# Attention and two gated MLPs on one core: three token blocks of 704, 768 and 832 in place of 768 each

## The chip, the core and the metric

The kernel runs on one core of a Trainium2 chip. The metric is device time in microseconds (us), the median of the runs shown. The core has five engines that run their own instruction streams and wait for one another by semaphores: PE (matmul), DVE (vector), ACT (scalar), POOL (general) and SP, which here issues almost every DMA, in program order.

## The reference

Attention over 4 batches x 8 heads of 576 queries and keys, head size 64, with a threshold: scores below the row's maximum minus tau are dropped before the softmax. Its output is reshaped to 2304 tokens x 512, and two gated MLPs (the code calls them moe) follow, the first with an RMS normalisation in front:

```python
scores = scale * (q @ k.T)
scores = where(scores >= max(scores) - tau, scores, -1e9)
x = softmax(scores) @ v                      # -> 2304 x 512
x = mlp(rmsnorm(x) * rms_g); x = mlp(x)
# mlp: g = x @ w_gate; (g * sigmoid(g) * (x @ w_val)) @ w_out,  512 -> 1536 -> 512
```

## The kernel before

**Tokens and blocks.** The kernel holds everything transposed: features on partitions, tokens along the free dimension. The 2304 tokens (batch by batch, 576 each) go in three blocks of 768. A block needs all 8 heads of its tokens, so `PHASES` cuts the queries: block 0 takes batch 0 and the first 192 queries of batch 1, block 1 the other 384 of batch 1 and 384 of batch 2, block 2 the rest. For each of four head pairs and each such piece the queries of both heads are laid end to end and cut into tiles of 128 rows (`queries`, `PLAN`): 48 tiles per block. Where a head's rows are no multiple of 128, one tile serves two heads.

**Two attention paths.** Block 0's tiles go first and alone, on a quick path (`fast`): products in plain f32, softmax on DVE, ACT and POOL, transposes on PE, product with V. It works in steps of two tiles (128 queries of either head) or, at the end of a piece whose length is an odd multiple of 64, one tile of 64 queries of either head. The tiles of blocks 1 and 2 (`tile_ops`, `pv`) run beside the MLPs on a split path: q, k and v are cut into parts whose products PE takes at full rate, the probabilities are written as two f16 halves, transposed by DMA, and multiplied with V in groups of query columns (`GROUPS`), nine full products and six of half height per group.

**MLPs.** Per block and MLP there are 18 weight units: 12 of gate and value columns (`gate_val`) and 6 of output columns (`outp`). Every product is made of three products of split parts, so a unit is 48 matmuls of half a block's width HT = 384 columns (`dense`, L923). In the last block 22 of the 24 gate-and-value units use a scheme with seven products in place of eight (`gate_val7`, L955; weights in `weights7`), which needs eight combinations of the activations (`combine`), kept in buffers that earlier served attention (`TS`).

**Weights.** In block 0 they come as 64-bit numbers and are converted on ACT and DVE and split (`weights`, `w_split`). They are then stored in DRAM for the later blocks, either as both parts (1024 KB) or, for units in `K_E`, as the unsplit f32 (512 KB) that is split again on reload. Units of the seven-product scheme need the unsplit copy as well.

**Order.** The program's operations are collected with a cost, a due time and their dependences, and a list scheduler (`order`) writes out the order for each engine. Due times come from constants (`T0`, `UP`, `FP`, `OFF`, `OFFF`, `LEAD` ...); tables such as `NORM_E`, `HI_E`, `V_E`, `H_E` say which engine takes an operation. On the chip each engine runs its list strictly in order. `Ring` hands out a buffer's slots in turn; a slot's new user waits for the old ones. Between the blocks `rms` sums the squares on PE (L739), computes 1/rms on DVE, spreads it over partitions (L762), and `norm` and `put` write the MLP's split input.

Of the kernel before, what the change touches and what calls it, by code (L numbers as in the profile page):

```python
# [46 lines left out]
PHASES = [[(0, 0, 576), (1, 0, 192)], [(1, 192, 384), (2, 0, 384)], [(2, 384, 192), (3, 0, 576)]]  # L47
# [3 lines left out]
    384: [(0, 0, 384), (1, 0, 384)],  # L51
    192: [(0, 0, 192), (1, 0, 192)],
# [32 lines left out]
NORM_E = [(1, 0, 0, 1, 1, 0, 0, 1, 1, 1, 0, 1), (1, 1, 1, 1, 0, 2, 0, 1, 2, 1, 1, 1), (1, 0, 2, 1, 0, 0, 0, 1, 1, 0, 2, 0)]  # L85
HI_E = [(1, 2, 1, 1, 0, 0, 0, 2, 2, 0, 0, 1), (2, 1, 0, 1, 0, 1, 0, 0, 1, 2, 2, 0), (1, 0, 2, 1, 0, 1, 0, 0, 1, 0, 1, 0)]
LO_E = [(0, 0, 0, 0, 0, 0, 0, 2, 2, 0, 2, 2), (0, 0, 2, 0, 2, 2, 0, 0, 0, 0, 0, 0), (2, 0, 0, 0, 2, 0, 0, 2, 2, 2, 0, 0)]


V_E = {1, 3, 6, 7, 8, 12, 14, 15, 16, 21, 24, 27, 28, 29, 30, 31, 32, 34, 37, 38, 39, 40, 44, 46, 47, 48, 51, 53, 55, 56, 58, 59, 61}  # L90
K_E = {1, 3, 6, 7, 8, 12, 14, 18, 19, 20, 22, 24, 25, 26, 30, 31, 32, 33, 34}
W_E = {1, 2, 3, 131, 133, 6, 8, 137, 138, 11, 12, 13, 14, 139, 16, 17, 18, 19, 141, 21, 143, 25, 27, 29, 30, 31, 33, 35, 37, 42, 44, 45, 47, 49, 52, 54, 55, 56, 58, 59, 60, 61, 65, 67, 69, 75, 76, 77, 82, 84, 86, 89, 92, 96, 97, 101, 103, 104, 105, 106, 108, 110, 111, 113, 114, 117, 120, 121, 122, 125}
H_E = {0, 1, 2, 4, 5, 8, 11, 12, 14, 15, 18, 20, 21, 23, 24, 25, 27, 28, 30, 31, 32, 35, 37, 38, 39, 42, 43, 44, 46, 47, 49, 50, 51, 55, 56, 57, 58, 59, 60, 61, 62, 63, 66, 67, 69, 70, 71, 73, 74, 80, 84, 85, 87, 88, 93, 94, 95}
X_E = {2, 6, 10, 11, 14, 15, 16, 18, 21, 24, 25, 29, 31, 32, 33, 34, 35, 39, 40, 41, 43, 44, 46, 48, 51, 54, 57, 58, 59, 61, 62}
P_E = {0, 1, 2, 3, 4, 6, 7, 8, 9, 10, 15, 16, 17, 19, 23, 25, 28, 29, 30}

# [150 lines left out]
def body(ctx: ExitStack, tc: tile.TileContext, qkv, tau, w1, rg, w2, outT):  # L247
# [13 lines left out]
    def ring(name, n, shape, dt):  # L261
        return Ring([sb.tile(shape, dt, name=f"{name}{i}") for i in range(n)])
# [67 lines left out]
    r_v3 = Ring([take(160).bitcast(BF16).rearrange("p (c d) -> p c d", c=5) for _ in range(3)])  # L330
# [6 lines left out]
    r_ag = Ring([take(9 * 192).bitcast(F16).rearrange("p (c q) -> p c q", c=9) for _ in range(3)])  # L337
    TMP = [take(384) for _ in range(2)]
    SQ = take(384)
# [19 lines left out]
    def retire():  # L359
        ops = {pg.wrote[k] for k in ("SQ",)} | {i for r in [r_raw2, r_x, r_v, r_v3, r_e, r_ep, r_e16, r_ag, *r_tmp] for b in r.slots for i in b.ops}  # L360
# [6 lines left out]
    r_tok = Ring([small[:, 6 * i:6 * i + 6] for i in range(3)])  # L367
    COL = sb.tile([P, 70], F32, name="col")
    r_col = Ring([COL[:, 14 * i:14 * i + 14] for i in range(5)])


    def SU(u):

        full = 36 * (NB - 1)
        if u <= full:
            return T0 + u * UP
# [830 lines left out]
```

## Time and profile before

| | |
|---|---|
| median of 3 runs | 1155.95 us (1155.9 to 1157.87) |
| the profiled execution | 1156.71 us, span 1154.7 us |
| PE busy | 1129.3 us, 98% of the span |
| DVE, ACT, POOL busy | 833.4, 687.4, 639.4 us |
| DMA | 186.72 MB moved, mean 162 GB/s |
| first split-path tile on PE | 145.0 us |

The span runs from the first to the last instruction of the profiled execution; the execution's own time is 2.0 us longer. A row of the timeline gives start, duration and form of one run of like instructions. Matmuls overlap, so the distance between two starts is what a run of them takes of PE.

### The profile page before, as it was taken

What the parts mean: (1) busy time and instruction counts of PE and PEld (TensorE: products, weight loads), DVE (VectorE), ACT (ScalarE), POOL (GpSimd) and SP (SyncE); (2) the same over time, 40 slices, a digit from 0 to 9 for tenths busy, and PEclk for the clock granted to TensorE, in tenths of its full rate; (3) what the DMA queues carried; (4) which work ended last, traced back from release to release, by engine and by line L of the source; (5) the groups of instructions that cost most, each with busy time, mean ns of one, the idle gap of its engine ahead of it and who ended that gap; (6) DMA issues with size and microseconds to landing.
All of it is one profiled execution on the core that took longest, in us unless ns stands there. A gap on an engine that the chain in (4) does not pass through costs nothing.

```text
span 1154.7 us, 19332 instructions
## 1 busy us (share of the span) xinstructions
PE 1129.3 (98%) x7176; PEld 1052.7 (91%) x7176; DVE 833.4 (72%) x1492; ACT 687.4 (60%) x972; POOL 639.4 (55%) x772
## 2 busy tenths in 40 slices
PE   7989999999999999999999999999999999999998
PEld 5656899889989998999999999999999999999998
DVE  7999488788978787787667557646587476884754
ACT  5798588888798887645644444544343353544531
POOL 5577145867678786756675674563152653453610
PEclk8999999999999999999999999999999999999999
DMA  5563349999888899857675545554343222122111
GB/s 180 174 202 140 100 159 256 273 276 283 243 259 244 262 265 235 222 200 179 150 187 153 161 123 138 134 135 107 76 167 144 91 74 91 55 93 90 38 55 55
DMA packets 174429, 186.72 MB, mean 162 GB/s; under 512 B 143872, under 2 KB 147712, under 8 KB 163968
## 3 DMA queue, kind: packets, MB, share of 16 engines
q1 hardware_dynamic: 174048, 185.50, 55.5%
q8 instruction: 56, 0.92, 0.3%
q14 instruction: 37, 0.30, 0.1%
q10 hardware_dynamic: 288, 0.00, 0.0%
HBM read 121.51 MB, written 35.65 MB: 136 GB/s over the span
## 4 chain that ended last, share of the span: by engine, by line
PE 81%; DVE 5%; ACT 4%; DMA 4%; issue 3%; POOL 3%; SPq 0%; POOLq 0%; ACTq 0%; DVEq 0%
PE ps L923 52%; PE pb L955 12%; PE ps L662 4%; PE pt L711 4%; PE ps L955 2%; PE pt L618 2%; DMA arena<-arena 2%; PE ps L558 2%; PE pt L597 1%; PE pt L713 1%; DVE col L571 1%; DMA arena<-in_qkv 1%; ACT arena L644 1%; ACT arena L502 0%; POOL arena L521 0%
## 5 line engine op out<-in xcount | busy, mean ns | idle before, releaser
L923 PE MATMUL ps<-XS,w 128*128 128x384 f32 x2400 | 439.2, 338 | 1.2 <-DVE th L1021 0.8
L923 PEld LDWEIGHTS ps<-XS,w 128*128 128x128 f32 x2400 | 414.1, 189 | 8.1 <-issue 4.6
L923 PE MATMUL ps<-h,w 128*128 128x384 f32 x1704 | 311.7, 337 | 0.5 <-DVE th L1032 0.4
L923 PEld LDWEIGHTS ps<-h,w 128*128 128x128 f32 x1704 | 296.5, 188 | 3.9 <-issue 1.6
L676 DVE TENSOR_REDUCE col<-ps 128x1 f32<-128x576 f32 x96 | 72.4, 754 | 59.1 <-PE ps L662 58.6
L679 DVE SCALAR_TENSOR_TENSOR arena<-ps,col,arena 128x576 f32<-128x576 f32 x96 | 78.0, 813 | 34.0 <-ACT arena L678 32.6
L678 ACT ACTIVATE arena<-ps,col 128x576 f32<-128x576 f32 x96 | 70.8, 738 | 51.9 <-DVE col L677 44.5
L955 PE MATMUL pb<-rx,arena 128*128 128x384 f32 x352 | 100.2, 339 | 0.0
L1039 ACT CAST h<-th 128x768 fp32r<-128x768 f32 x72 | 60.1, 834 | 67.3 <-DVE th L1032 35.4
L893 POOL TENSOR_TENSOR arena<-w,arena 128x384 fp32r<-128x384 f32 (+1 forms) x52 | 65.7, 1285 | 51.4 <-ACT arena L891 47.9
L521 POOL TENSOR_TENSOR arena<-arena 128x512 f16<-128x512 f32 x68 | 86.0, 1266 | 0.0
L828 POOL TENSOR_TENSOR w<-w,w 128x1024 fp32r<-128x1024 f32 x25 | 60.7, 2427 | 44.9 <-ACT w L826 44.7
L1043 POOL TENSOR_TENSOR h<-th,h 128x768 fp32r<-128x768 f32 (+1 forms) x32 | 51.5, 1615 | 58.3 <-ACT h L1039 58.0
L826 ACT CAST w<-w 128x1024 fp32r<-128x1024 f32 x58 | 60.9, 1050 | 37.9 <-PE ps L923 25.9
L662 PE MATMUL ps<-rx 128*128 128x288 f32 x416 | 71.4, 296 | 3.9 <-DVE arena L679 3.9
L662 PEld LDWEIGHTS ps<-rx 128*128 128x128 f32 x416 | 63.7, 188 | 6.6 <-DVE arena L679 3.6
L502 ACT ACTIVATE arena<-arena,col 128x576 f32<-128x576 f32 x68 | 58.3, 865 | 18.7 <-DVE col L689 17.2
L1021 DVE SCALAR_TENSOR_TENSOR th<-th,ps 128x768 f32<-128x768 f32 x48 | 45.6, 951 | 29.7 <-ACT th L1020 27.3
L1084 DVE SCALAR_TENSOR_TENSOR Y<-ps,Y 128x768 f32<-128x768 f32 x47 | 44.7, 955 | 29.5 <-PE ps L923 29.2
L965 ACT COPY X<-pb 128x384 f32<-128x384 f32 x66 | 31.4, 478 | 57.0 <-PE pb L955 57.0
L955 PEld LDWEIGHTS pb<-rx,arena 128*128 128x128 f32 x352 | 64.5, 188 | 0.1
L1043 DVE TENSOR_TENSOR h<-th,h 128x768 fp32r<-128x768 f32 x47 | 55.6, 1186 | 8.9 <-ACT h L1039 8.9
(166 smaller groups left out, 2026.4 us busy)
## 6 DMA issues: line engine op xcount, KB each, us to landing
w<-in_w SPq DMA_DIRECT2D x36, 1024.0 KB, 6.3
w<-kept SPq DMA_DIRECT2D x28, 1024.0 KB, 5.1
w<-kept SPq DMA_DIRECT2D x44, 512.0 KB, 3.8
kept<-w SPq DMA_DIRECT2D x17, 1024.0 KB, 5.2
kept<-w SPq DMA_DIRECT2D x25, 512.0 KB, 3.8
arena<-in_qkv SPq DMA_DIRECT2D x40, 160.0 KB, 3.2
ra<-in_qkv SPq DMA_DIRECT2D x10, 576.0 KB, 3.9
out<-Y SPq DMA_DIRECT2D x11, 384.0 KB, 2.6
```

The lines of the kernel that those rows point to most:

```text
L521: op(en, 601 if eng == 2 else 1128, lambda: n1.tensor_tensor(h[:, 640:], e[:, :512], h[:, :512], ALU.subtract), lock=True, w=[("lo", n)], ...
L662: nc.tensor.matmul(s[:, j, :HS], x[:, c:c + P], x[:, k:k + HS], start=i + u == 0, stop=i == 1 and u == len(heads) - 1)
L676: op("DVE", 670, lambda: nc.vector.tensor_reduce(c[:, 0:1], s2, AX.XY, ALU.max, negate=True), w=[*sk, ("mx", n)], bufs=[cb], p=T + F['MAX' ...
L678: op("ACT", 640, lambda: nc.scalar.activation(e2, s2, AF.Exp, bias=c[:, 2:3], scale=SCALE), r=[("thr", n)], w=[*sk, ("e", n)] + ek, bufs=[ ...
L679: op("DVE", 750, lambda: nc.vector.scalar_tensor_tensor(e2, s2, c[:, 1:2], e2, ALU.is_ge, ALU.mult, accum_out=c[:, 6:7]), r=[("thr", n)], ...
L826: op("ACT", 939, lambda: nc.scalar.copy(ws[:, 0], w), r=[("w32", n)], w=[("wh", n)], bufs=[b32, sbf], p=p, name=f"w_split{n}")
L828: op(en, 1142 if en == "DVE" else 2340, lambda: n1.tensor_tensor(ws[:, 1], w, f32(ws[:, 0]), ALU.subtract), lock=True, r=[("w32", n), ("wh ...
L893: op(en, 70 + (z - a) * 105 // 100 if en == "DVE" else 190 + (z - a) * 210 // 100, lambda a=a, z=z: n2.tensor_tensor(sbf.t()[:, 1, a:z], s ...
L923: nc.tensor.matmul(pt[:, j, :HT], w(i, a), x(i, b_)[:, j * HT:(j + 1) * HT], start=(i == 0 and a == 0 and b_ == 0), stop=(i == n - 1 and a ...
L955: nc.tensor.matmul(bank(), w()[:, a, col * 256 + i * P:][:, :P], xf(i, b_), start=first and i == 0 and a == 0 and b_ == 0, stop=i == 1 and ...
L1039: op("ACT", 734, lambda: nc.scalar.copy(h[:, 0], tb.t), r=[("th", n)], w=[("h0", n)], bufs=[tb, hb], p=p + OFF['HH'], name=f"h{n}")
L1043: op(eng, 72 + (z - a) * 105 // 100 if eng == "DVE" else 190 + (z - a) * 209 // 100, lambda a=a, z=z: n1.tensor_tensor(h[:, 1, a:z], tb.t[ ...
```

## The change

The blocks become 704, 768 and 832 tokens. Tiles are sized for 832 and used by the block's width; pieces, groups and tile counts (44, 48 and 52) follow. The tables of engines and the constants of the due times are all new (left out here, but for the rows where a constant was added). Squares are summed over 256 + 320 + 128 columns in place of 384 + 192 + 192. A unit's split parts are rebuilt later only if it is in `K_E` and also among the seven-product units (`keeps`): 13 units in place of 19. V's third part has two buffers in place of three, the temporary of `pv` one in place of two, and two of the eight combination buffers move from the old attention arena to the ring of unsplit weights, for whose users `retire` now waits too.

```diff
-NB, TW = 3, 768
+NB, TW = 3, 832
 HT = TW // 2
+TWB = (704, 768, 832)
+T0B = (0, 704, 1472)
-NTC = 12
-NTB = NP * NTC
+NTC = (11, 12, 13)
+NTB = NP * NTC[0]
+END = (44, 92, 144)
-PHASES = [[(0, 0, 576), (1, 0, 192)], [(1, 192, 384), (2, 0, 384)], [(2, 384, 192), (3, 0, 576)]]
+PHASES = [[(0, 0, 576), (1, 0, 128)], [(1, 128, 448), (2, 0, 320)], [(2, 320, 256), (3, 0, 576)]]
 GROUPS = {
     576: [(0, 0, 256), (0, 256, 320), (1, 0, 320), (1, 320, 256)],
-    384: [(0, 0, 384), (1, 0, 384)],
-    192: [(0, 0, 192), (1, 0, 192)],
+    448: [(0, 0, 256), (0, 256, 192), (1, 0, 192), (1, 192, 256)],
+    320: [(0, 0, 320), (1, 0, 320)],
+    256: [(0, 0, 256), (1, 0, 256)],
+    128: [(0, 0, 128), (1, 0, 128)],
 }
-ARENA = 12768
+ARENA = 11232
-UP, FP, T0, DRAIN, ATT, LEAD, LEAD2, UL, RMS0, RMS1, CREL = 10544, 1362, 179133, -12670, 22274, 8, 8, 9919, -50718, -149645, 80130
+UP, UP0, FP, T0, DRAIN, ATT, LEAD, LEAD2, UL, RMS0, RMS1, CREL = 10845, 9605, 125, 161144, -15067, 24701, 9, 8, 8318, 139285, -294364, 74416
+def block(n):
+    b = sum(n >= e for e in END)
+    return b, n - (END[b - 1] if b else 0)
+def pattern(table, n):
+    b, i = block(n)
+    return table[2 - b][i % 13]
+def keeps(i):
+    return i in K_E and i in GV
...
-    r_v3 = Ring([take(160)... for _ in range(3)])
+    r_v3 = Ring([take(160)... for _ in range(2)])
-    r_ag = Ring([take(9 * 192)... for _ in range(3)])
-    TMP = [take(384) for _ in range(2)]
-    SQ = take(384)
+    r_ag = Ring([take(9 * 160)... for _ in range(3)])
+    TMP = [take(320)]
+    SQ = take(320)
...
     def TS(a, k):
-        t, o = (again("rx", 2 * XW), i) if i < 4 else (again("ra", 4 * S), i - 4) if i < 7 else (again("arena", ARENA)[:, 3 * 3584:], 0)
+        t, o = (again("rx", 2 * XW), i) if i < 4 else (again("ra", 4 * S), i - 4) if i < 6 else (again(f"w32{i - 6}", 1024), 0)
...
     def SU(u):
-        full = 36 * (NB - 1)
-        if u <= full:
-            return T0 + u * UP
-        return T0 + full * UP + sum(...)
+        t = T0 + min(u, 2 * NU) * UP0 + min(max(u - 2 * NU, 0), 2 * NU) * UP
+        if u > 4 * NU:
+            t += sum(...)
+        return t
...
     def rms(b):
-            for t in range(6):
-                nc.tensor.matmul(p[:, 2 * t:2 * t + 2], SS[:, t * P:(t + 1) * P], ones, start=True, stop=True)
+        cuts = [min(t * P, TW - P) for t in range(-(-TW // P))]
+            for t, a in enumerate(cuts):
+                nc.tensor.matmul(p[:, 2 * t:2 * t + 2], SS[:, a:a + P], ones, start=True, stop=True)
...
-            if i in K_E:
+            if keeps(i):
...
-        if n in K_E:
+        if keeps(n):
...
-    def dense(pt, pk, n, w, x, wkeys, xkeys, bufs, T, U):
+    def dense(pt, pk, n, w, x, wkeys, xkeys, bufs, T, U, HT):
...
     def moe(b, between):
+        TW = TWB[b]
+        HT = TW // 2
```

## Rows read from the trace of the kernel before

**Rows 1.** Engine busy time by stage: window, length, busy per engine, granted clock, DMA share, GB/s.

```profile
16.00:128.40 112.40, 103.75 (x1029) 71.40 (x1028) 92.46 (x210) 88.33 (x166) 69.62 (x142) 0.99 0.48 158
128.40:500.00 371.60, 364.15 (x2172) 340.96 (x2171) 302.92 (x503) 300.06 (x365) 246.35 (x288) 1.00 0.86 244
500.00:875.00 375.00, 374.45 (x2357) 358.17 (x2356) 253.21 (x517) 175.69 (x258) 205.62 (x222) 1.00 0.54 145
875.00:1151.40 276.40, 276.40 (x1581) 276.04 (x1579) 175.21 (x246) 116.36 (x172) 110.60 (x92) 1.00 0.21 73
```

**Rows 2.** Who PE waited for over the whole span: total, times, longest.

```profile
PE ps L662 <- DVE arena L679: 3.9, 4, 1.6
...
PE pt L711 <- DMA arena<-arena: 2.4, 3, 1.3
```

**Rows 3.** PE in order of time, first stage: start, duration, instruction, count.

```profile
91.66 0.66 PE L597 MATMUL pt<-ident,Y 128*128 128x128 f32 x4
92.15 0.27 PE L602 MATMUL pt<-ident,arena 128*128 128x128 f32 x1
92.36 0.76 PE L558 MATMUL ps<-rx 64*128 64x288 f32 x4
93.04 0.95 PE L618 MATMUL pt<-arena 128*64 128x64 f32 x20
93.92 0.33 PE L602 MATMUL pt<-ident,Y 128*128 128x128 f32 x1
...
101.83 0.71 PE L558 MATMUL ps<-rx 64*64 64x288 f32 x8
...
102.50 0.66 PE L597 MATMUL pt<-ident,arena 128*128 128x128 f32 x4
```

**Rows 4.** PE in order of time, split path in blocks 0 and 1.

```profile
145.01 0.69 PE L662 MATMUL ps<-rx 128*128 128x288 f32 x4
145.53 0.68 PE L923 MATMUL ps<-XS,w 128*128 128x384 f32 x3
...
183.85 1.64 PE L711 MATMUL pt<-arena 128*128 128x384 f16 x9
185.42 0.60 PE L713 MATMUL pt<-arena 128*64 128x192 f16 x6
185.94 0.44 PE L923 MATMUL ps<-XS,w 128*128 128x384 f32 x1
...
528.55 0.92 PE L711 MATMUL pt<-arena 128*128 128x192 f16 x9
529.40 0.40 PE L713 MATMUL pt<-arena 128*64 128x96 f16 x6
529.73 0.44 PE L923 MATMUL ps<-XS,w 128*128 128x384 f32 x1
```

**Rows 5.** PE in order of time, the spread before the last block.

```profile
855.05 1.50 PE L762 MATMUL ps<-ident,small 128*128 128x128 f32 x12
```

**Rows 6.** DMA issues of the whole span: count, KB each, median us to landing.

```profile
kept<-w SPq DMA_DIRECT2D x17, 1024.0 KB, 5.2
kept<-w SPq DMA_DIRECT2D x25, 512.0 KB, 3.8
```

**Rows 7.** Engine busy time within block 0, columns as in rows 1.

```profile
232.00:300.00 68.00, 67.42 (x402) 63.17 (x401) 58.45 (x96) 55.43 (x68) 45.45 (x59) 1.00 0.97 282
300.00:400.00 100.00, 97.28 (x582) 90.25 (x582) 79.22 (x129) 87.59 (x107) 76.25 (x85) 1.00 0.85 251
400.00:500.00 100.00, 98.22 (x596) 91.61 (x595) 80.76 (x138) 69.36 (x84) 69.21 (x84) 1.00 0.92 242
```

**Rows 8.** POOL's groups of instructions, 130 to 500 us: busy, mean ns, idle before.

```profile
L487 POOL TENSOR_TENSOR arena<-arena 128x320 f32<-128x320 f32 (+1 forms) x19 | 19.0, 998 | 15.0 <-DMA arena<-in_qkv 8.8 <-PE ps L923 4.2 <-DVE col L689 1.1
...
L726 POOL TENSOR_TENSOR X<-X,arena 64x384 f32<-64x384 f32 x8 | 8.5, 1062 | 8.2 <-ACT X L725 8.0
```

**Rows 9.** Engine busy time at the first normalisation, columns as in rows 1.

```profile
128.00:136.00 8.00, 7.56 (x48) 6.78 (x45) 4.72 (x16) 6.31 (x9) 0.72 (x1) 0.79 0.10 24
```

More of the change, by code (lines that the diff above doesn't have):

```diff
@@ L261, in ring @@
     def ring(name, n, shape, dt):
-        return Ring([sb.tile(shape, dt, name=f"{name}{i}") for i in range(n)])
+        return Ring([sb.tile(shape, dt, name=f"{name}{i}", tag=f"{name}{i}") for i in range(n)])
     PB, PD = [ps.tile([P, 2, 512], F32, name=f"ps{i}") for i in range(2)]
@@ L329, in body @@
     r_v = Ring([take(10 * D).rearrange("p (c a d) -> p c a d", c=5, a=2) for _ in range(3)])
-    r_v3 = Ring([take(160).bitcast(BF16).rearrange("p (c d) -> p c d", c=5) for _ in range(3)])
+    r_v3 = Ring([take(160).bitcast(BF16).rearrange("p (c d) -> p c d", c=5) for _ in range(2)])
     ET = take(4 * S).rearrange("p (i s) -> p i s", i=4)
@@ L336, in body @@
     r_e16 = Ring([take(S).bitcast(F16) for _ in range(3)])
-    r_ag = Ring([take(9 * 192).bitcast(F16).rearrange("p (c q) -> p c q", c=9) for _ in range(3)])
-    TMP = [take(384) for _ in range(2)]
-    SQ = take(384)
+    r_ag = Ring([take(9 * 160).bitcast(F16).rearrange("p (c q) -> p c q", c=9) for _ in range(3)])
+    TMP = [take(320)]
+    SQ = take(320)
     r_tmp = [Ring([t[h:h + 64] for t in TMP]) for h in (0, 64)]
@@ L365, in retire @@
             b.ops = xbuf.ops
-    r_tok = Ring([small[:, 6 * i:6 * i + 6] for i in range(3)])
     COL = sb.tile([P, 70], F32, name="col")
+    TOK = sb.tile([P, 21], F32, name="tok")
+    r_tok = Ring([TOK[:, 7 * i:7 * i + 7] for i in range(3)])
     r_col = Ring([COL[:, 14 * i:14 * i + 14] for i in range(5)])
     def SU(u):
-        full = 36 * (NB - 1)
-        if u <= full:
-            return T0 + u * UP
-        return T0 + full * UP + sum(UL * (0.875 if i in GV else 1.0) for i in range(u - full))
+        t = T0 + min(u, 2 * NU) * UP0 + min(max(u - 2 * NU, 0), 2 * NU) * UP
+        if u > 4 * NU:
+            t += sum(UL * (0.875 if i in GV else 1.0) for i in range(u - 4 * NU))
+        return t
     def ST(n):
@@ L680, in tile_ops @@
         cc = lambda i: c[:, i:i + 1]
-        se = S_E[1 if n < 2 * NTB else 0]
+        se = S_E[2 - block(n)[0]]
         ns = nc.gpsimd if se == 0 else nc.vector
@@ L715, in pv @@
         op("PE", int(9 * (w * 0.422 + 1) + 5 * w * 0.2145 + 190), PV, r=keys + [("v1", hd), ("v2", hd), ("v3", hd)], w=[vk], bufs=[ab, v, v3], p=T, name=f"PV{n}")
-        last = c == NP - 1 and q0 + w == TW and hp
+        last = c == NP - 1 and q0 + w == TWB[b] and hp
         m = m0 = 64 * hp
@@ L760, in spread @@
         def spread():
[L761 to L762 removed]
+            for t, a in enumerate(cuts):
+                nc.tensor.matmul(full[:, a:a + P], y[:, t:t + 1].to_broadcast([P, P]), ident, start=True, stop=True)
         if b:
[L765 removed]
+            tiles(min(END[b] + RL, END[-1]))
         op("PE", 1400, spread, r=[("rm", b)], w=BK["PA"], bufs=[yb], p=T, name=f"rms_spread{b}", cols=0)
         if b == 0:
[L768 removed]
+            op("ACT", 710, lambda: nc.scalar.copy(RB[:, :TW], full[:, :TW]), w=BK["PA"] + SK(0, TW), p=T, name="rms_spread0")
         for c in range(NC):
[L770 to L771 removed]
+            x = X[:, c, :TW]
+            op("DVE", 110 + TW * 105 // 100, lambda c=c, x=x: nc.vector.scalar_tensor_tensor(x, x, rgs[:, c:c + 1], full[:, :TW] if b else RB[:, :TW], ALU.mult, ALU.mult),
                lock=b == 0, r=["rg"] + ([] if b else SK(0, TW)), w=(BK["PA"] if b else []) + [("Xn", b, c)] + XK(c, 0, TW), p=T, name=f"norm{c}")
@@ L777, in norm @@
         for c in range(NC):
-            put(c, X[:, c], [("Xn", b, c)] + XK(c, 0, TW), [xbuf] if last else [], T, ("POOL", "DVE")[8 * b + c in P_E])
+            put(b, c, X[:, c, :TWB[b]], [("Xn", b, c)] + XK(c, 0, TWB[b]), [xbuf] if last else [], T, ("POOL", "DVE")[8 * b + c in P_E])
         if last:
@@ L821, in body @@
     w64, w32, wsp = {}, {}, {}
-    kept2 = {i: dr.tile([P, 1024], F32, name=f"kept2_{i}") for i in GV if i not in K_E}
+    kept2 = {i: dr.tile([P, 1024], F32, name=f"kept2_{i}") for i in GV if not keeps(i)}
     kept = [dr.tile([P, 2, 1024], F32, name=f"kept{i}") for i in range(2 * NU)]
@@ L1099, in moe @@
                     norm(0)
-                    tiles(2 * NTB)
+                    tiles(END[1])
                 if f == 3:
@@ L1141, in body @@
     for c in range(NP):
-        tiles(NTC * (c + 1))
+        tiles(NTC[0] * (c + 1))
         put_raw(c)
@@ L1153, in body @@
         if 0 < b < NB - 1:
-            tiles((b + 2) * NTB)
+            tiles(END[b + 1])
         moe(b, between)
```

158 lines of the change are left out of this document (79 added, 79 removed).

## The prediction

> **What bounds the kernel now.** I read the profile from the whole to the place: busy time by stage, PE's waits, PE's instructions in order of time, and last the load of the queue and of the other engines. By stage [rows 1] the reader should see four different states of PE. In the attention-only stage (16 to 128.4 us) PE is busy for 103.75 of 112.4 us and three engines are close to one another. In block 0 it idles 7.45 us in 371.6, in block 1 0.55 us in 375, in block 2 not at all. The waits [rows 2] say what those idle microseconds are: queries times keys waits for the mask on DVE, and attention times V for a DMA transpose. From 16 us on the time is therefore PE's instruction stream plus 16.6 us of holes, and a change is worth what it does to that stream, plus what it does to the holes. Work taken from DVE, ACT or POOL in blocks 1 and 2 is worth nothing.
>
> Durations of single matmuls overlap, so I price PE work by the distance between the starts of successive rows of its timeline.
>
> **Part 1: the first stage loses one step per head pair.** With 192 further query columns in block 0 each of the four head pairs had a last step of one tile that mixes 64 rows of either head; with 128 columns that step is gone (48 tiles become 44). The step costs [rows 3]: queries times keys 0.67 us (101.83 to 102.50), five transposes 0.70 us (91.66 to 92.36), its product with V 0.88 us (93.04 to 93.92). That is 2.25 us, and four of them are 9.0 us of PE. It takes with it four tiles of DVE and ACT work, so that neither of these takes PE's place. The stage's holes (8.65 us, [rows 1]) stand between the steps; in proportion to PE's work (9.0 of 103.75 us) 0.8 us of them go too. At the low end they all stay (9.0), at the high end twice as many go (10.6).
>
> **Part 2: the removed queries come back on the split path.** Queries times keys there takes four matmuls per tile and head, 0.52 us (145.01 to 145.53, [rows 4]). Before: 96 tiles and 8 that serve two heads, 104 sets. After: 100 tiles and 12 that serve two heads (448 and 320 columns leave one each per head pair in place of none in 384; 256 leaves none in place of one in 192), 112 sets. Eight sets: +4.2 us. The products with V, in groups of columns: 192 columns take 0.85 + 0.33 = 1.18 us, 384 take 1.57 + 0.52 = 2.09 us [rows 4]; straight between them 256 take 1.48 and 320 take 1.79. Before: 16 groups of 384, 8 each of 192, 256, 320, together 69.0 us. After: 24 of 256, 8 of 192, 16 of 320, together 73.6 us: +4.6 us. In block 0 alone these two are +4.2 and +2.2 us (eight sets; 35.6 against 33.4 us). All of it is in PE's stream, and nothing hides it.
>
> **Part 3: the seven-product scheme gets 64 tokens more.** The tokens of ordinary units only move between blocks: 1728 matmuls per block, 32 columns shorter in block 0 and 32 longer in block 2, same count. The 22 units with seven products in place of eight save 6 matmuls each, and these now are 416 columns wide in place of 384: 22 x 6 x 32 = 4224 columns less. From 192 to 384 columns nine matmuls grow by 0.72 us [rows 4], 0.417 ns a column: -1.8 us.
>
> **Part 4: the normalisation.** A seventh cut in the last block adds two matmuls to the sums and two to the spread; twelve spread matmuls last 1.50 us [rows 5], so at most 0.25 us each: +0.5 us.
>
> **Part 5: weights.** Units whose split parts are rebuilt later from the stored weights become 13 in place of 19. That takes nine casts from ACT and nine subtractions from DVE and POOL, all in blocks 1 and 2, where PE has 0.55 us of holes: between 0 and -0.5, I take 0. It costs stores: 17 of 1024 KB and 25 of 512 KB [rows 6] become 23 and 22, that is 4.72 MB more, in block 0, where DMA is fullest, and six more half-megabyte loads in block 1, where its share is 0.54. In block 2 a share of 0.21 moves 73 GB/s [rows 1], so a megabyte costs 2.9 us of all 16 DMA engines: 13.6 us of queue time in block 0. On the path I take +1.0 us of holes for it and for the shorter block, of which rival C says more; from zero to +7.
>
> **Part 6: rings and places.** One temporary per half in place of two makes ACT's copy out of PSUM wait for the addition before it (POOL, 1.06 us, [rows 8]); such groups lie some ten microseconds apart in PE's stream and use alternate banks: 0, at most one such addition late, +1. Two buffers for V's third part: the subtraction for the next pair (1.00 us, [rows 8]) waits for the last product of the pair before, and its own first product comes only after tiles of its own have been transposed: 0, at most +1 per pair boundary, 8 in all. Two of the eight combination buffers move into the weight ring: the ring's last user is a unit that PE multiplies before the combination starts: 0. DVE's, ACT's and POOL's widths in a block scale with PE's: 0.
>
> **The sum.** -9.0 - 0.8 + 4.2 + 4.6 - 1.8 + 0.5 + 1.0 = -1.3. The new engine choices and orders can move PE's holes by a microsecond or two in either direction; since less work in the first stage leaves more room for the same buffers, I put -0.5 there. That gives -1.8 us. The profiled execution took 1156.71 us (span 1154.7 and 2.0 around it), 0.8 above the median of the runs shown, 1155.95; the difference carries over, so 1154.1 on the runs' scale. A measurement of this kernel can tell about 0.2%, 2.3 us, from no change: the forecast lies inside, near the edge at 1153.6.
>
> **Rival B: the first stage closes up.** With all steps alike (pairs of whole tiles, but one) and new due times, half of its 8.65 us of holes go. After 128 us the granted clock is 0.79 over 8 us [rows 9], a stretch at the lower level (1.2 GHz) that comes after transposes and small products with waits between them; full clock there is worth 8 x 0.21 = 1.7 us. Together 1.8 + 4.3 + 1.7 less the 0.8 and 0.5 that the forecast already has: -6.5, or 1149.5. For it: the holes wait on ACT and DVE copies, not on data. Against it: DVE and ACT are at 92 and 88 of 112 us, and the end of the stage, a product, a copy, the sums, stays a chain.
>
> **Rival C: DMA sets the pace of block 0.** PE's stream in block 0 shrinks by 36 units x 48 matmuls x 32 columns x 0.417 ns = 23.0 us and grows by 6.4: 371.6 becomes 355.0. The queue's work does not shrink with it: 0.86 x 371.6 = 319.6 us, plus 13.6, is 333.2, a share of 0.94. From 400 to 500 us the share was 0.92 and from 232 to 300 us 0.97 [rows 7]. If the queue can hold no more than 0.92 over the block, the block takes 362.2 us: +7.2, of which the sum already has 1.0, so 1160.3. It decides from the point at which the weights of a unit land after the unit before it has ended; every PE instruction behind stands still then. The same pressure falls on ACT (300 of 371.6 us, which becomes about 297 of 355). For it: all engines but PE get a fuller block. Against it: from 232 to 300 us PE lost only 0.6 us of 68 at a share of 0.97, and stores can wait while loads pass.
> On 358 GB/s of HBM bandwidth per core the Trainium skill ("DMA: Bandwidth & Descriptors", Specifications) would call this harmless: 244 GB/s over 371.6 us and 4.7 MB more are 269 GB/s, three quarters of it, and C would have a twentieth. The rows show the engines full at 282 GB/s [rows 7], much of it in small packets of the transposes, and the measurement decides.
>
> **Rival D: the gain goes back into holes.** From 300 to 400 us, with ACT at 87.6 of 100, PE lost 2.7% [rows 7]. If the whole shorter block 0 runs at that rate it loses 9.6 us in place of 7.45, and the V ring costs one late product (1.0): 3.2, of which 1.0 is already in the sum: 1156.3. For it: block 0 is the only place where the other engines get tighter. Against it: the lost waits are only nine, and other orders may miss them.
>
> **How the numbers follow.** Forecast 1154.1 with its own range 1152.3 to 1155.9: 0.42, of which 0.17 lies below 1153.6. B 0.25, all of it below. D 0.13, no change. C 0.20, slower (1158.3 and more). Faster 0.17 + 0.25 = 0.42; within 0.2% 0.25 + 0.13 = 0.38; slower 0.20. The range goes from 1148.0 (B with the rest of the first stage's holes partly gone) to 1161.0 (C and a little), which leaves out about a fifth: the half of C that is dearer than its price, and a small part of B.
>
> **What the new profile would show.** Right, if the sums of squares of block 0 are multiplied some 9 to 11 us earlier than 128.4 us, if block 0 then takes about 356 us, block 1 about 377 (eight groups of 256 columns in place of 192: +2.4) and block 2 about 21 us longer (36 units, 1596 matmuls x 32 columns x 0.417 ns), and if PE has 112 sets at the split queries-times-keys line. B: under 5 us of PE holes before the first normalisation, and granted clock 1.0 behind it. C: PE waiting for the weight splits' loads or for DMA transposes for more than 8 us in block 0, and a DMA share of 0.92 and more there. D: PE holes of 10 us in block 0, ended by DVE's mask. The sum would be wrong if block 1, which has no holes to give, differed from that by more than 2 us: then a price of part 2 is wrong.

## The result: slower, with block 0 hardly shorter than before

The changed kernel took 1168.26 us (median; 1166.79 to 1169.11, 4 runs) against 1156.11 for the kernel before on the same chip: ratio 1.0092, 95% interval 1.008 to 1.0104, so 12 us slower where 1.8 faster was forecast. The profiled execution took 1169.11 us, its span 1167.3.

First the changed kernel's busy time by the stages of [rows 1]: attention only, then blocks 0, 1 and 2. Columns: stretch, its length, busy us (instructions) of PE, PE's weight loads, DVE, ACT and POOL, granted clock, DMA share, GB/s.

```profile
16.00:116.86 100.86, 94.04 (x887) 63.70 (x885) 82.33 (x190) 80.46 (x147) 64.32 (x128) 0.98 0.49 163
116.86:488.69 371.83, 357.28 (x2335) 336.51 (x2333) 307.46 (x506) 298.72 (x383) 251.92 (x294) 0.98 0.91 258
488.69:861.41 372.72, 372.72 (x2334) 355.33 (x2333) 265.74 (x556) 165.38 (x243) 213.34 (x233) 1.00 0.56 155
861.41:1163.70 302.29, 302.27 (x1597) 298.36 (x1596) 182.34 (x234) 120.20 (x170) 128.66 (x108) 1.00 0.22 77
```

Here and below a stage is cut at the same instruction in every kernel: the first matmul of block 0's sums of squares, then the first gate matmul of blocks 1 and 2; before, that is at 128.36, 501.22 and 872.11 us, and block 2 is taken to 1151.41. [Rows 1] have the cuts at round numbers, so their lengths differ a little. The forecast column is what the prediction gave for each stage.

| stage | before | after | change | forecast |
|---|---|---|---|---|
| up to block 0 | 128.36 | 116.86 | -11.5 | -9.8 |
| block 0 | 372.86 | 371.83 | -1.0 | -15.6 |
| block 1 | 370.89 | 372.72 | +1.8 | +2.4 |
| block 2 | 279.30 | 302.29 | +23.0 | +21.3 |

The first and the last stage are near the forecast, block 0 is not: it gives 1.0 us where 15.6 were expected. That is the whole miss (14.6 us, where the span missed by 14.4; the rest cancels). PE's holes in it went from 7.45 us to 371.83 - 357.28 = 14.55. PE's longest waits in block 0, with total us, times and longest, to be set against [rows 2]:

```profile
PE ps L684 <- DVE arena L701: 6.6, 9, 2.0
PE pt L733 <- DMA arena<-arena: 4.9, 4, 1.8
PE ps L950 <- DVE w L855: 1.6, 1, 1.6
```

The same two waits lead (queries times keys for the mask, product with V for a DMA transpose), and a new one stands behind them: a unit that waits for its split weights. PE in order of time shows three of them close together, the idle time and what ended it in brackets:

```profile
253.31 0.80 PE L684 MATMUL ps<-rx 128*128 128x288 f32 x4 [0.27 <-DVE arena L701]
255.92 0.90 PE L733 MATMUL pt<-arena 128*128 128x192 f16 x9 [1.81 <-DMA arena<-arena]
256.76 0.40 PE L735 MATMUL pt<-arena 128*64 128x96 f16 x6
259.20 1.33 PE L684 MATMUL ps<-rx 128*128 128x288 f32 x4 [2.04 <-DVE arena L701]
```

The same place in windows, columns as above:

```profile
252.00:256.00 4.00, 1.92 (x12) 1.42 (x11) 4.00 (x7) 2.31 (x3) 3.56 (x6) 1.00 1.05 253
256.00:260.00 4.00, 1.96 (x18) 1.58 (x18) 3.34 (x7) 2.73 (x5) 2.05 (x4) 0.77 0.88 231
260.00:264.00 4.00, 3.75 (x14) 3.23 (x13) 3.23 (x6) 3.97 (x5) 1.37 (x1) 0.50 0.98 318
264.00:268.00 4.00, 4.00 (x25) 4.00 (x25) 2.04 (x4) 3.42 (x5) 3.74 (x3) 0.88 0.96 238
```

PE is busy half the time for 8 us, and meanwhile the granted clock falls to its lower level (1.2 GHz), where it stays for some 7 us: 4 x (0.23 + 0.50 + 0.12) = 3.4 us of full-speed time are lost. It is low again around the hole at 416 us and in the first normalisation. Added up in 4 us windows from 100 us to the end of block 0, the lower level cost 8.5 us, before 1.7. So block 0's PE stream (its length less holes and lost clock) did become shorter, 371.8 - 14.6 - 8.5 = 348.8 against 372.9 - 7.5 - 1.7 = 363.7, and holes and clock took 13.9 of the 14.9 us back. The experiments ask why.

### The profile page after: what moved, and what is told of

It reads as the page before. It is cut to its first block, busy times and chain, and to the rows that moved or that the text cites. A ratio compares the mean times of both kernels' runs of the same rounds, so it can differ in the third digit from the quotient of the medians.

```text
span 1167.3 us, 19383 instructions
## 1 busy us (share of the span) xinstructions
PE 1137.4 (97%) x7192; PEld 1060.9 (91%) x7192; DVE 848.0 (73%) x1505; ACT 672.3 (58%) x953; POOL 665.9 (57%) x790
## 4 chain that ended last, share of the span: by engine, by line
PE 73%; ACT 8%; DVE 6%; DMA 5%; POOL 4%; issue 3%; SPq 0%; ACTq 0%; POOLq 0%; DVEq 0%
PE ps L950 45%; PE pb L985 13%; PE ps L684 3%; PE pt L733 3%; PE ps L985 2%; DMA arena<-arena 2%; DMA kept<-w 2%; PE pt L640 2%; PE ps L580 1%; PE pt L619 1%; ACT w L891 1%; PE pt L735 1%; ACT t L893 1%; ACT arena L700 1%; DVE w L894 1%
## 5 line engine op out<-in xcount | busy, mean ns | idle before, releaser
L950 PE MATMUL ps<-XS,w 128*128 128x352 f32 (+2 forms) x2400 | 427.6, 334 | 1.2 <-DVE th L1051 0.9
L950 PE MATMUL ps<-h,w 128*128 128x352 f32 (+2 forms) x1704 | 313.3, 338 | 1.8 <-DVE w L855 1.6
L985 PE MATMUL pb<-rx,arena 128*128 128x416 f32 x352 | 105.2, 351 | 0.0
L1069 ACT CAST h<-th 128x704 fp32r<-128x704 f32 (+2 forms) x72 | 60.0, 833 | 74.7 <-DVE th L1019 43.0
L1073 POOL TENSOR_TENSOR h<-th,h 128x416 fp32r<-128x416 f32 (+2 forms) x35 | 57.5, 1645 | 79.4 <-ACT h L1069 79.2
L1051 DVE SCALAR_TENSOR_TENSOR th<-th,ps 128x768 f32<-128x768 f32 (+2 forms) x48 | 44.4, 924 | 36.9 <-ACT th L1050 36.8
L1114 DVE SCALAR_TENSOR_TENSOR Y<-ps,Y 128x704 f32<-128x704 f32 (+2 forms) x47 | 44.7, 952 | 34.4 <-PE ps L950 33.9
L853 ACT CAST w<-w 128x1024 fp32r<-128x1024 f32 x49 | 51.3, 1047 | 29.3 <-PE ps L950 14.9
L1062 DVE SCALAR_TENSOR_TENSOR th<-th,ps 128x768 f32<-128x768 f32 (+2 forms) x48 | 44.3, 924 | 25.8 <-PE ps L950 25.5
L995 ACT COPY X<-pb 128x416 f32<-128x416 f32 x66 | 33.0, 504 | 51.3 <-PE pb L985 51.3
L733 PE MATMUL pt<-arena 128*128 128x256 f16 (+2 forms) x432 | 57.5, 278 | 4.9 <-DMA arena<-arena 4.9
L1050 ACT ACTIVATE th<-ps 128x768 f32<-128x768 f32 (+2 forms) x48 | 37.8, 787 | 41.6 <-PE ps L950 41.4
```

Source lines behind the costliest of these rows:

```text
L733: nc.tensor.matmul(pv_[:, :w], v12[:, i if i < 5 else i - 5], o[:, i, :w], start=(i == 0), stop=False)
L853: op("ACT", 939, lambda: nc.scalar.copy(ws[:, 0], w), r=[("w32", n)], w=[("wh", n)], bufs=[b32, sbf], p=p, name=f"w_split{n}")
L950: nc.tensor.matmul(pt[:, j, :HT], w(i, a), x(i, b_)[:, j * HT:(j + 1) * HT], start=(i == 0 and a == 0 and b_ == 0), stop=(i == n - 1 and a ...
L985: nc.tensor.matmul(bank(), w()[:, a, col * 256 + i * P:][:, :P], xf(i, b_), start=first and i == 0 and a == 0 and b_ == 0, stop=i == 1 and ...
L1069: op("ACT", sbuf, lambda: nc.scalar.copy(h[:, 0, :TW], tb.t[:, :TW]), r=[("th", n)], w=[("h0", n)], bufs=[tb, hb], p=p + OFF['HH'], name=f ...
L1073: op(eng, 72 + (z - a) * 105 // 100 if eng == "DVE" else 190 + (z - a) * 209 // 100, lambda a=a, z=z: n1.tensor_tensor(h[:, 1, a:z], tb.t[ ...
```

## The experiments

Each edit but the two orders keeps every engine's order. The code shows the main line of an edit. "Block 0" is its length, to be set against 372.86 (before) and 371.83 (after); ratios are to the kernel before on the same chip, with 95% intervals.

### One engine or queue eased at a time

**a_stores.** 23 stores and the reloads of both split parts move 128 of 1024 columns.

```
- dma_start(kept[n], f32(ws))
+ dma_start(kept[n][:, :, :128], f32(ws)[:, :, :128])        # the reload likewise
```

> The changed kernel, every engine's order kept, but the 23 stores of both split parts in block 0 move 128 of 1024 columns (and their reloads too): some 21 MB, about 60 us of queue time, gone from block 0. The later blocks then multiply weights that are partly old, so the output is not the reference's. Theory DMA (the fuller queue makes stores and transposes land late, conversions and products wait, PE's holes and the low clock behind them follow): block 0 falls from 371.8 to about 360 us, the run to 1155 to 1159. Rival order (the order written for these blocks leaves ACT and DVE late whatever the queue does): 1165 to 1168. Rival rings (V's third part or the single temporary): 1165 to 1168.

1165.25 us, 1.0063 (1.0045 to 1.0081); block 0 367.87, DMA share 0.76 in place of 0.91. Some 3 to 4 us come back, not the loss.

**a_hold.** The 22 stores of one part read the rounded part from the split buffer, so that the 32-bit buffer is not held for them.

```
- dma_start(kept[n][:, 0], w)
+ dma_start(kept[n][:, 0], f32(ws)[:, 0])
```

> The changed kernel, order kept, the same bytes stored, but the 22 stores of unsplit weights read the first split part instead (the stored values differ a little from the reference's), so that the ring of two unsplit buffers is freed by the split's subtraction and not by a store's landing. Theory DMA by holding (ACT's first conversion waits for a store to land: 8.4 us in five waits): 1158 to 1163. Theory DMA by traffic alone, rivals order and rings: within 2 us of 1168.

1167.90 us, 1.0082 (1.0065 to 1.0098); block 0 371.84. Holding the 32-bit buffer for these stores costs nothing.

**a_conv.** ACT's three conversion passes work on 128 of 1024 columns.

```
- activation(q, top, AF.Prelu, ...)
+ activation(q[:, :128], top[:, :128], AF.Prelu, ...)   # the other two likewise
```

> The changed kernel, order and DMA kept, but ACT's three conversion passes of every unit take 128 of 1024 columns, some 3.3 us less of ACT per unit, 115 us in block 0 (the weights are then wrong). Rival order/ACT (ACT's and DVE's chain is what is late): block 0 falls to 358 to 362 us, the run to 1155 to 1159. Theory DMA: the stores still land late and are waited for, at most a third of it comes back, 1163 to 1167.

1163.42 us, 1.0049 (1.0032 to 1.0066); block 0 366.07. ACT's load falls from 299 to 220 us there (by 79, where 115 were expected), and 5 to 6 us come back.

**a_both.** a_stores and a_conv in one.

> The changed kernel, order kept, with both earlier reliefs: the stores of both parts and the three conversion passes on ACT take 128 of 1024 columns (weights wrong). Rival two limits (DMA and ACT take turns, each relief alone shows only the other): block 0 at 356 to 361 us, the run 10 us and more under the changed kernel. Theory score chain, which neither relief touches: no better than the ACT relief alone by more than 3 us, 1160 to 1164.

1161.47 us, 1.0032 (1.002 to 1.0044); block 0 363.72. About the sum of the two, 7 to 8 us, and PE still has 8.8 us of holes, the largest at the same places (near 252, 256 and 411 us). The time lies in the range given for the score chain, but the next run speaks against that chain.

**a_score.** Maximum and mask, the operations PE is seen waiting for, on 128 of 576 columns.

```
- tensor_reduce(c[:, 0:1], s2, AX.XY, ALU.max, negate=True)
+ tensor_reduce(c[:, 0:1], s2[:, :, :64], AX.XY, ALU.max, negate=True)   # the mask likewise
```

> The changed kernel, order kept, but on the split path the row maximum and the mask with its sum take 128 of 576 columns (the softmax is then wrong): 0.94 us less of DVE per tile, 45 us in block 0, all of it between the scores in PSUM and the next tile's product. Theory score chain (one pair of PSUM banks holds a tile's scores; the next product waits for the mask, and the shorter block leaves each tile less time): block 0 at 360 us or less, the run 8 to 12 us under the changed kernel, 1155 to 1160. Rival DVE load: 4 to 7 us under it. Rival DMA: within 2 us of it.

1168.64 us, 1.0089 (1.0067 to 1.0112); block 0 371.99. DVE is 47 us lighter in block 0, and the waits only change their name: 3.7 us for the mask and 8.1 us for the DMA transposes, where it was 6.6 and 4.9. The operation that ends a wait is here not what sets its length.

**a_dve.** DVE's joining pass on 128 of 1024 columns from the fifth conversion on.

```
- scalar_tensor_tensor(w, mid, 13, bb.t, ...)
+ scalar_tensor_tensor(w[:, :z], mid[:, :z], 13, bb.t[:, :z], ...)   # z = 128
```

> The changed kernel, order kept, but DVE's joining pass of the weight conversion takes 128 of 1024 columns from the fifth unit on (the weights are then wrong): some 1.15 us less of DVE per unit, 37 us in block 0, none of it between a tile's scores and the next product. Theory score chain: at most 4 us under the changed kernel. Rival DVE load: 4 to 7 us under it, as in the kernel with the shorter maximum and mask.

1168.41 us, 1.0091 (1.006 to 1.0121); block 0 373.40. DVE's load alone isn't it.

### The kernel before with one part of the change's load

**b_twice.** Nine of its half-megabyte stores are made twice, 4.7 MB more in block 0, as the change does.

> The kernel before, order kept, with nine more stores of 512 KB in block 0 (4.7 MB, the growth of the changed kernel's stores; nobody reads them). Theory DMA: block 0's share rises from 0.86 to about 0.90, PE's holes grow, 1159 to 1166. Rivals order and rings: 1156 to 1158.

1162.52 us, 1.0038 (1.0022 to 1.0054); block 0 377.78, 5 us longer. In the old order those stores cost 5 us.

**b_ring2.** V's third part in two buffers, one temporary per half.

> The kernel before, order kept, with two buffers for V's third part in place of three and one temporary per half in place of two (same results, waits added where the order does not already keep them apart). Rival rings: 1159 and more, the rings cost a good part of what the changed kernel lost. All other theories: 1156 to 1158.5, as before.

1158.00 us, 1.001 (1.0 to 1.0019); block 0 371.35. In the old order the rings cost about a microsecond, at most 2.2, and block 0 is no longer for it. What they cost in the new order no run shows.

### The holes, the clock and the order

**a_fill.** Identity matmuls ahead of the three instructions behind the largest holes, into unused columns of the score bank. The ten at the third place came in twice, so there are 46 in all.

```
+ for _ in range(k):
+     matmul(PA[:, 0, 384:], ident, ident, start=True, stop=True)
```

> The changed kernel with 36 idle-time matmuls (identity by identity, 128 columns, into unused columns of the score bank) ahead of the three PE instructions behind the largest holes of block 0: 12 ahead of the product with V that waited 1.81 us for a DMA transpose at 255.9 us, 14 ahead of the queries times keys that waited 2.04 us for the mask at 259.2, 10 ahead of the unit that waited 1.58 us for its weights at 418.1. Nothing else is changed, each engine's order included. Clock theory (each big hole is followed by some microseconds at the lower clock level, which cost 3.4 us at 256 to 268 and 1.7 us at 416 to 424): the holes are filled, the granted clock there is 1.00, and the time is 3 to 5 us less, 1163 to 1165. Rival, the low clock belongs to the place and not to the hole before it, or the hole itself is all the loss: same time, 1167 to 1169, or up to 3 us more if the added matmuls come late.

1180.24 us, 1.0197 (1.0175 to 1.0218). The matmuls waited for the maximum and the mask on that bank themselves and came behind the holes (12 of them are recorded as 24):

```profile
254.23 2.94 PE L306 MATMUL ps<-ident 128*128 128x128 f32 x24 [1.14 <-DVE col L703]
260.29 5.02 PE L306 MATMUL ps<-ident 128*128 128x128 f32 x28 [2.04 <-DVE arena L706]
```

So this run tells nothing of the clock. It does tell that PE work put before a score costs: 46 x 0.245 = 11.3 us of it made block 0 9.1 us longer (380.92).

**a_warm.** The same into columns of the product's own bank, free at once: 7 ahead of that product with V and 8 behind it, 6 behind the one before 418 us.

> The changed kernel with identity matmuls (245 ns each in a_fill) into unused columns of the product's own bank, ready as soon as PE reaches them: 7 ahead of the product with V that waited 1.81 us at 255.9 us, 8 behind it (a wait of 2.04 us follows), 6 behind the product ahead of the unit that waited 1.58 us for its weights at 418. Clock theory: PE stays busy over 252 to 262 and 414 to 420, the granted clock stays at 1.00 there, and the time is 3 to 5 us less, 1163 to 1165.5. Rival, it only adds work or the clock falls all the same: 1167 to 1172.

1175.26 us, 1.0146 (1.0128 to 1.0165); block 0 379.08. PE in order of time:

```profile
255.91 1.72 PE L306 MATMUL pt<-ident 128*128 128x128 f32 x14
257.91 0.92 PE L738 MATMUL pt<-arena 128*128 128x192 f16 x9 [0.27 <-DMA arena<-arena]
259.08 2.05 PE L306 MATMUL pt<-ident 128*128 128x128 f32 x16
263.17 0.80 PE L688 MATMUL ps<-rx 128*128 128x288 f32 x4 [2.04 <-DVE arena L705]
```

The first hole was filled, but behind the second filling the wait of 2.04 us stands as before, only 4 us later, and the low clock with it (0.83 over 262 to 272). The mask that PE waits for comes later when PE does, and 21 matmuls of 0.245 us, 5.1 us of work, made block 0 7.3 us longer. So PE's own place in the order is part of what these holes wait for; I take it to be a loop through PE's small products, which no run isolates. What the low clock costs by itself stays open.

**a_ord2, a_ord3.** The changed blocks with other due times and engine choices, so other orders, and with one more store of both parts (24 of 1024 KB).

```
- UP, UP0, FP, T0, ... = 10845, 9605, 125, 161144, ...
+ ...   # other values here, in OFF, OFFF and the tables of engine choices
```

> The changed kernel's blocks, rings and units, with other engine choices and due times, so another order on every engine; taken because the list that the kernel's own scheduler writes with them leaves PE fewer holes in block 0. Order theory (the loss of block 0 is made by the order written for it): block 0 comes from 371.8 us to 362 to 368, PE's holes there under 11 us, the time 1160 to 1165. Rival, capacity (the shorter block has too little room for the same conversions, transposes and stores on ACT and DMA, whatever their order): block 0 stays within 2 us of 371.8 and the time at 1166 to 1170.

> A second other order of the same blocks, found on its own from another start, with still fewer planned holes of PE in block 0 and a first stage some 3 us longer. Order theory: first stage and block 0 together end 4 to 9 us earlier than 488.7, the time 1158 to 1164. Capacity theory: they end within 2 us of 488.7 and the time is 1166 to 1170.

a_ord2 1178.56 us, 1.0162 (1.0138 to 1.0185), block 0 374.05; a_ord3 1172.75, 1.0123 (1.0102 to 1.0145). Block 0 of a_ord3:

```profile
116.04:487.94 371.90, 356.58 (x2331) 334.38 (x2329) 298.92 (x506) 293.71 (x374) 245.48 (x294) 0.98 0.92 255
```

371.90 us again; what made the run longer is block 1 (378 us, with 4 us of holes). On block 0 the capacity side was right, in a_ord2 by 0.2 us beyond its 2 us; both times lie above every range given. a_ord3 is a neighbour of the given order (it issues the transfers of 205 to 260 us in nearly the same sequence). a_ord2 is farther off: its sequence of transfers in block 0 agrees with the changed kernel's in about half the places. Both are the work of the same scheduler, so two orders do not rule out a better one.

### PE's work against the pace of the rest

**b_narrow, a_narrow.** 40 columns less in 36 of the 48 matmuls of each unit of block 0, in either kernel.

```
- pt[:, j, :HT], w(i, a), x(i, b_)[:, j * HT:(j + 1) * HT]
+ pt[:, j, :hn if i else HT], w(i, a), x(i, b_)[:, j * HT:j * HT + (hn if i else HT)]   # hn = HT - 40
```

> The kernel before, with 40 of 384 columns left out of 36 of the 48 matmuls of each of block 0's 36 units: 1296 matmuls, each some 18 us per thousand shorter (175 ns at 384, 160.4 ns at 352 columns, so 18.2 ns), 23.6 us less of PE work in block 0, about what the change takes from it. Every order and all work of the other engines stay. Pace theory (the other engines and the queue need some 365 to 372 us for block 0 whatever PE does): block 0 goes from 372.9 to 362 to 369 us, PE's holes there from 7 to over 17 us, the time to 1147 to 1154. Order theory (only the order written for the changed blocks is bad): block 0 falls by most of it, to 350 to 355 us, and the time to 1134 to 1140.

> The changed kernel with the same edit: 40 of 352 columns left out of 36 of 48 matmuls of block 0's units, 23.6 us less of PE work. Pace theory: block 0 has no more to give; 371.8 goes to 365 to 372, the time to 1162 to 1169, with 30 us of holes and more at the lower clock. Order theory, with PE as the pace between a few holes: block 0 falls to 348 to 356 us, the time to 1145 to 1153.

b_narrow 1156.58 us, 0.9991 (0.9982 to 1.0); a_narrow 1167.45, 1.0087 (1.0073 to 1.0101). Block 0 of b_narrow, then of a_narrow:

```profile
129.19:501.32 372.13, 353.82 (x2181) 323.71 (x2177) 304.35 (x503) 301.10 (x366) 246.68 (x288) 0.98 0.86 244
```

```profile
116.71:488.53 371.82, 341.60 (x2334) 315.41 (x2333) 301.75 (x507) 298.48 (x383) 254.17 (x294) 0.97 0.90 256
```

This decides it. The time of block 0 doesn't move: 372.9 and 372.1, 371.8 and 371.8, while PE's holes grow to 18.3 and 30.2 us. By length less holes and lost clock PE's stream fell by 16.7 and 19.1 us (23.6 were expected); in b_narrow 10.9 of the 16.7 went into holes and 5.1 into lower clock. So shortening PE's big products does not shorten block 0, in the kernel before either. b_narrow came out slower than even the pace theory's range (block 0 362 to 369, time to 1154), a_narrow inside it. What PE waits for in b_narrow is again the mask (7.2 us) and the DMA transposes (6.8); its wait for weights is 0.4 us.

### The stream of weights

**a_light, b_light.** In either kernel block 0's stream of weights at an eighth from the fifth conversion on: load, conversion and joining passes, cast, subtraction, stores and reloads of both parts. The stores of one part stay whole, and the three conversion passes are cut in all 36 units.

```
- dma_start(t[:, 1:4097], ...bitcast(U16))
+ dma_start(t[:, 1:z + 1], ...bitcast(U16)[:, :z])        # z = 512
- scalar.copy(ws[:, 0], w)
+ scalar.copy(ws[:, 0, :z], w[:, :z])                     # z = 128, and the other passes
```

> The changed kernel with the whole stream of weights of block 0 at an eighth from its fifth conversion on (load, three conversion passes, joining pass, cast, subtraction, and the stores and reloads of both parts); attention, PE and all orders stay. a_both, with the conversion passes and stores alone, gave 1161.5 and a block 0 of 363.7. If the weights set the pace: block 0 at 350 to 358 us, under 5 us of PE holes, the time 1146 to 1155. If the attention chain (scores, mask, transposes, product with V) in its order sets it: no more than 2 us beyond a_both, block 0 at 361 or more, the time 1159 or more.

> The kernel before with the edit of a_light: block 0's loads, conversion and joining passes, casts and subtractions, and the stores and reloads of both parts at an eighth from the fifth conversion on. Same pace in both kernels: block 0 falls from 372.9 to 361 to 367 us, the time to 1147 to 1152, so that a_light (1154.85) is no faster than it, and the loss of PE work in block 0 is what the change gives away. If instead only the changed kernel is held by the weights: block 0 stays at 370 us and more, the time at 1154 to 1158, and a_light equals it or is up to 3 us better, as the sum of PE's terms said (-1.8).

a_light 1154.85 us, 0.9976 (0.9967 to 0.9985); b_light 1147.71, 0.9918 (0.9903 to 0.9933). Block 0 of a_light, then of b_light:

```profile
117.08:475.35 358.27, 353.14 (x2334) 335.81 (x2333) 245.86 (x506) 195.51 (x383) 196.66 (x294) 0.98 0.51 129
```

```profile
127.12:492.24 365.12, 363.95 (x2181) 342.35 (x2178) 249.99 (x504) 196.48 (x366) 188.55 (x288) 1.00 0.51 131
```

With light weights block 0 of the changed kernel falls by 13.6 us and that of the kernel before by 7.7. b_light's 365 us are PE's, with 1.2 us of holes; the 7.7 us that the kernel before has above that go with the load of the weights. The changed kernel's PE stream is 358.3 less 5.1 of holes and 6.8 of low clock, 346.3, against 362.2 in b_light by the same sum: 15.9 us less, which no run of the full stream could show as time. Even so a_light's time stays 7.1 us behind b_light's: in block 0 it has 3.9 us more of holes (mainly 1.35 and 2.05 us, near 252 and 256 us) and 5.1 us more of lost clock.

**a_dma, a_eng.** The two halves of a_light: the transfers of both parts and the loads alone, and the passes of the engines alone.

> The changed kernel with the transfers of the stream of weights alone at an eighth (loads from the fifth unit on, stores and reloads of both parts); the stores of one part and all passes of the engines stay. If the queue is the part that holds block 0: 1155 to 1160, near a_light. If the passes of the engines are: 1162 to 1166, near a_stores (1165.25).

> The changed kernel with the passes of the stream of weights alone at an eighth (three conversion passes, joining pass, cast, subtraction); all transfers stay. If the passes are the part that holds block 0: 1155 to 1159, near a_light. If the queue is: 1162 to 1166. If it takes both, as with a_conv (-4.8) and a_stores (-3.0), which gave -6.8 together: this and a_dma both lie at 1158 to 1163.

a_dma 1162.14 us, 1.004 (1.0026 to 1.0055), block 0 366.51; a_eng 1163.61, 1.0056 (1.0036 to 1.0077), block 0 367.62:

```profile
115.88:482.39 366.51, 354.46 (x2335) 334.43 (x2333) 305.90 (x506) 299.04 (x383) 254.94 (x294) 0.98 0.49 126
```

```profile
116.50:484.12 367.62, 353.36 (x2335) 334.00 (x2333) 249.36 (x506) 195.65 (x383) 197.28 (x294) 0.99 0.92 260
```

5.3 us at a DMA share of 0.49, 4.2 us with ACT and DVE a third and a fifth lighter, and 13.6 together: more than the sum of 9.5, so either half alone holds block 0 when the other is eased. The ranges do not tell: a_dma lies in the one for "it takes both" and a_eng 0.6 us above it, but each also lies in the range by which the other half alone would be the cause. It is the 13.6 that tells.

## Why the prediction was wrong

**The step that failed** stands in the first paragraph: "the time is therefore PE's instruction stream plus 16.6 us of holes, and a change is worth what it does to that stream, plus what it does to the holes", with the +1.0 us of part 5 as all that the holes would take back. In block 0 the two are no separate terms. The stream became 14.9 us shorter, and holes and low clock (for which the sum had nothing) took 13.9 us of it back. The rows showed PE busy 98% of block 0 [rows 1, 7], and I read that as PE setting the time. b_narrow shows that in the kernel before too a shorter stream shortens nothing: beside PE's path, some 365 us long (b_light), stands another of some 372 us, which runs mostly through the other engines and the queue.

The traces of the two kernels already hold this. The profile follows the chain of work that ended last back through what released each instruction (releasers are inferred). These are its shares of block 0, line by line, before, after and in b_light; the view ends each line where it does here:

```profile
by line: PE ps L923 54.7%; PE pt L711 5.7%; PE ps L662 5.3%; issue 4.0%; DMA arena<-arena 4.0%; PE pt L713 1.8%; DMA arena<-in_qkv 1.6%; DMA w<-in_w 1.3%; DVE th L1021 1.2%; ACT w L826 1.1%; DVE arena L679 1.1%; DVE X L771 1.0%; DVE col L67
```

```profile
by line: PE ps L950 24.4%; issue 7.3%; DMA arena<-arena 6.3%; DMA kept<-w 5.1%; ACT w L891 3.3%; ACT t L893 3.3%; PE ps L684 2.8%; PE pt L733 2.7%; ACT arena L700 2.6%; DVE w L894 2.6%; ACT w L853 2.6%; ACT w L892 2.1%; POOL arena L543 1.9%
```

```profile
by line: PE ps L924 80.1%; PE ps L662 7.3%; PE pt L711 6.5%; PE pt L713 2.3%; PE ps L762 0.9%; DMA arena<-in_qkv 0.7%; issue 0.4%; PE pt L739 0.3%; DVE arena L679 0.2%; DVE col L676 0.2%; ACT arena L678 0.2%; POOL arena L487 0.2%; DVE small
```

PE's lines here add up to 67.5% before, though PE was busy 98% of that block, to 29.9% after (31.2% in b_narrow) and to 97.4% in b_light. What stands between them after the change is work for the weights (stores, conversion and joining passes, casts) and for attention (DMA transposes, exponentials, the split on POOL), in turns. The load of the weights is shown to be what can be eased (a_light, b_light); that weights themselves come late is not, for PE hardly waits for them (1.9 us after, 0.4 in b_narrow). Nor does their spacing show it. The joining pass comes every 10.4 us before, every 10.6 us after and every 10.2 us in b_light, where PE sets the time: this is the block's length shared out among 36 units, whoever sets it.

Moving 64 tokens from block 0 to block 2 therefore saved 1.0 us in block 0 and cost 23.0 us in block 2.

**Part 5 and rival C.** Rival C had the right place and side, at 0.20, and 1160.3 was too low. I priced it by the DMA share alone and let block 0 shrink until the queue was at 0.92; the share was 0.91 (0.97 from 289 us on) and the block shrank by 1.0 us. a_dma shows that the share is not the whole price: with the queue at 0.49 only 5 us come back, since the passes of the engines still hold the block. Of C's sign, over 8 us of waits for weights or transposes, 6.8 us came (4.9, 1.6 and 0.3). My argument against C, that PE lost only 0.6 of 68 us at a share of 0.97, looked at PE's holes, which say nothing about a second path of nearly the same length. The other half of it, that stores can wait while loads pass, the traces speak against: of 71 transfers that SP issued while a store of weights was on its way in the kernel before, none landed before that store (after, none of 87). By the Trainium skill's 358 GB/s ("DMA: Bandwidth & Descriptors", Specifications) the queue would have had room at 258 GB/s; b_twice, 5 us longer at 251 GB/s and a share of 0.89, speaks against that. The stores' count was right, their landing became slower:

```profile
kept<-w SPq DMA_DIRECT2D x23, 1024.0 KB, 5.5
kept<-w SPq DMA_DIRECT2D x22, 512.0 KB, 5.4
```

(median us to landing last; 5.2 and 3.8 in [rows 6]).

**Part 1** was right in kind: -11.5 us, of which 9.8 forecast; PE is busy 9.7 us less there (9.0 forecast) and idle 1.8 less (0.8). Rival B's signs did not come: 6.8 us of holes are left, and the clock behind them was 0.50 and 0.87 at 120 to 128 us. **Part 2** held: block 1, which has no holes, took 1.8 us more where 2.4 were forecast, PE has the 112 sets, and a_light against b_light has PE's stream in block 0 at -15.9 where the terms give -16.6. **The price of a column** in part 3 was too low for block 2, which grew by 23.0 us where 21.3 were forecast. The dense products of the last block, before and after, and their start to start (24 of them between two rows):

```profile
1145.00 4.32 PE L923 MATMUL ps<-h,w 128*128 128x384 f32 x24
1149.16 2.25 PE L1066 MATMUL pb<-h,w 128*128 128x384 f32 x12
```

```profile
1156.73 4.72 PE L950 MATMUL ps<-h,w 128*128 128x416 f32 x24
1161.28 2.42 PE L1096 MATMUL pb<-h,w 128*128 128x416 f32 x12
```

4.16 / 24 = 173.3 ns and 4.55 / 24 = 189.6 ns: 0.51 ns a column in these rows. Over the whole block, 23.0 us for 1596 x 32 columns, it is 0.45, where I had taken 0.417 from the products with V. **Part 6**: b_ring2 bears out V's ring and the temporary in the old order; in the new one they are not tested. **Rival D** named the holes (10 us, ended by the mask; 14.6 came, of which the mask ends 6.6) but not their cause.

Open are the loop by which the transfers and passes of weights and attention hold each other, and so why the length is so nearly the same in both kernels and their narrow runs, what the low clock costs by itself, and whether a better order of the same blocks could use PE's 15 us.

## What to carry to other kernels

An engine that is busy 98% of a stage need not set its time alone: when a second path is nearly as long, the busy share can't tell them apart, and shortening the busy engine gives nothing. Before work is moved out of a stage, read there how much of the profile's chain runs through the busy engine (here 67.5%, not 98%). The spacing of some other stream's work is no test, since it follows the length of the stage whoever sets it. The cheap test is a run in which the busy engine alone does less, with one in which the others do less beside it; here they would have shown the answer without any change to the blocks.

## What the runs showed of the hardware

Two 4 us windows with PE half busy went with some 7 us at the lower clock level (0.77, 0.50, 0.88 at 256 to 268 us). It was low at nearly the same place again in a_both, a_light, a_dma and a_ord3, and at 268 to 276 us in a_ord2; each such place lost 1.7 to 5.1 us of full-speed time. Whether the block would be shorter without it, no run shows. The dense products of the last block (128 partitions, form f32) took 173.3 ns from start to start at 384 columns and 189.6 at 416. No transfer that SP issued behind a store of weights landed before it (none of 71 before, none of 87 after).
